# The borders between the passes of an FFT convolution: which PSUM slots and engines x's tiles use, and where they stand among the last transforms and modes

## Chip, cores and metric

One NeuronCore of a Trainium2 chip runs the kernel. The metric is device microseconds of one execution, the median over several runs. The kernel before takes 376.1 us (three runs: 375.57, 376.10 and 376.31).

## The reference, cut to what matters

x has shape (8, 5696, 128), h (5696, 128). The first half is a causal long convolution over the 5696 positions, by FFTs of length L = 2 * 5696; the second keeps 64 modes of the result's own FFT, mixes the 128 channels in each, transforms back, adds and passes a residual ReLU layer:

```python
Yf = np.fft.rfft(x, n=L, axis=1) * np.fft.rfft(h, n=L, axis=0)[None]
x = np.fft.irfft(Yf, n=L, axis=1)[:, :S, :]
X = np.fft.rfft(x, axis=1)[:, :64]                       # complex, 64 modes
Y = einsum('bmd,mde->bme', X, w_r + 1j * w_i)            # written in real parts
u = x + np.fft.irfft(Y, n=S, axis=1)
return u + np.maximum(u @ w_ch, 0.0)
```

## The kernel before

**The work.** The eight sequences are handled in four passes of two (`g_` from 0 to 3). The transform of length L is split into steps that are all matmuls. The *first transform* of a pass is 32 **tiles of x** (`a_tile`, line 466): tile j takes four channels, one matmul for each (128x180 out, constants F against x), into two neighbouring PSUM banks, a *slot* named by its lower bank (0, 2, 4 or 6). One eviction then copies the slot's 128x720 results to the SBUF tensor As, scaled by 1/64: on ScalarE (ACT; line 320 in the profile) or on VectorE (DVE; line 324). Tile 31 is evicted by both engines, half each.

Then the pass runs 23 **ticks** of four frequency columns (`ticks`; the last tick, 22, has two columns). A tick has the second transform (`second`, 128x128 matmuls ps<-As,M, which need all of As), the product with h's spectrum (`products`: mostly a copy Xs on ScalarE and a multiplication U on VectorE), and, two ticks later, the **third transform** (`third`, line 643): for each of the two sequences b two matmuls (ps<-U,Wc) into one bank and a copy Zs or Zt on ScalarE (line 318), then a DMA to the HBM scratch zscr on SP's queue. Its banks rotate through 4, 5 and 6 (`ZBANK`, with a counter `ring2["z"]` that runs on through the whole kernel). Three ticks later the **modes** (`modes_of`, line 660) accumulate small matmuls (ps<-G,Zs) into bank 7 (`MB`). After the last modes two ScalarE copies XT (lines 739 to 742) drain bank 7.

**The border** (lines 722 to 754). The tiles of the next pass can start when the second transform of the last tick is through. At the end of a pass transforms 21 and 22 (NT - 2 and NT - 1) and modes 20, 21 and 22 are still to be done. Before, PE's order is: transform 21 (both sequences), tiles 0 and 1 (slots 0 and 2), transform 22, tile 2 (slot 0), modes 20, tile 3 (slot 4), modes 21, tile 4 (slot 2), modes 22, XT, then tiles 5 to 31 in slots 0, 4, 6, 2 in turn. x itself is already in SBUF: it is loaded by DMA on POOL's queue during the ticks (`x_load`, to Xt) and rearranged by VectorE (`x_place`, line 371, Xin<-Xt), the last of eight in tick 22.

**Which engine evicts a tile** is chosen by `share` (line 435), a running balance of costs (670 ns for ScalarE, 815 for VectorE), with hand-set amounts added at the border. With V for VectorE and A for ScalarE it gives, for tiles 0 to 30, the same string at each border:

```
before  VAVVAVAVAVAVAVAAVAVAVAVAAVAVAVA
```

**What orders the work.** Every engine runs its instructions in the order in which the code records them. A `Recorder` derives the waits: a matmul into a bank waits for the eviction of what was in it, an eviction for the last matmul of its slot. After odd tiles from 5 on, one piece of the weights w_r, w_i is copied in HBM (wscr<-in_moe_w_r, 14 in a border) by a DMA on POOL's queue that waits for that tile's eviction; in the last border also loads W of those weights. Behind tile 31 PE runs nine matmuls on constants (`idle`), into slot 2.

Of the kernel before, what the change touches and what calls it, by code (L numbers as in the profile page):

```python
# [4 lines left out]
P = 128  # L5
# [118 lines left out]
def bass_long_conv_fft__then__afno_spectral_mix_kernel(nc, x, h, moe_w_r, moe_w_i, moe_w_ch, out):  # L124
# [10 lines left out]
    NT = (NK + KT - 1) // KT  # L135
# [156 lines left out]
    def ap(t, row, p0, n, off, dims):  # L292
        return bass.AP(t, p0 * row + off, [[row, n]] + [list(d) for d in dims])
# [5 lines left out]
    def pv(bank, off, dims, p0=0, n=P):  # L299
        return bass.AP(ps, p0 * 4096 + bank * 512 + off, [[4096, n]] + [list(d) for d in dims])  # L300
# [5 lines left out]
    def bank(i):  # L306
        return ("bank", i)
# [3 lines left out]
    def evac(dst, src, reads, writes, scale=None, eng=None, after=()):  # L311
        e = eng
        if e is None:
            turn[0] ^= 1
            e = "scalar" if turn[0] else "vector"
        if e == "scalar":
            if scale is None:
                R.add(e, lambda h_: h_.copy(dst, src), reads, writes, after=after)  # L318
            else:
                R.add(e, lambda h_: h_.activation(dst, src, COPY, scale=scale), reads, writes, after=after)  # L320
        elif scale is None:
            R.add(e, lambda h_: h_.tensor_copy(dst, src), reads, writes, after=after)  # L322
        else:
            R.add(e, lambda h_: h_.tensor_scalar_mul(dst, src, scale), reads, writes, after=after)  # L324

    def dma(eng, dst, src, ring, reads=(), writes=(), after=()):
        R.add(eng, lambda h_: h_.dma_start(dst, src), reads, writes, ring=ring, after=after)  # L327

    def mm(o, l, r, st, sp, reads, writes):
        R.add("tensor", lambda h_: h_.matmul(o, l, r, start=st, stop=sp), reads, writes)  # L330
# [3 lines left out]
    def once(key, toks):  # L334
        if key in first:
            return []
        first[key] = 1
        return list(toks)

    ring2 = {}  # L340

    def turns(name, items):
        i = ring2.get(name, 0)
        ring2[name] = i + 1
        return items[i % len(items)]
# [29 lines left out]
    def w_pieces():  # L375
        out_ = []
        for ri, w in ((0, moe_w_r), (1, moe_w_i)):
            for m0 in range(0, M, MWP):
                out_.append((bass.AP(wd, (ri * M + m0) * D, [[2 * M * D, P], [D, MWP], [1, D]]),
                             bass.AP(w.tensor, w.offset + m0 * D * D, [[D, P], [D * D, MWP], [1, D]]),  # L380
                             "w", ("wd", ri, m0)))
        return out_

    MWP = 4
    wp = w_pieces()
# [34 lines left out]
    ZBANK = [4, 5, 6]  # L420
# [4 lines left out]
    def idle(n, b0, w=512):  # L425
        for i in range(n):
            mm(pv(b0 + i % 2, 0, [[1, w]]), f1_sb[:, 0:P], ap(f1_sb, 2 * NK, 0, P, 0, [[0, w // P], [1, P]]),
               True, True, [("f1",)], [bank(b0 + i % 2)])
# [3 lines left out]
    load = {"scalar": 0.0, "vector": 0.0}  # L432
    COST = {720: (670, 815), 1024: (910, 1130), 256: (280, 330)}

    def share(n):
        a, v = load["scalar"] + COST[n][0], load["vector"] + COST[n][1]
        e = "scalar" if a <= v else "vector"
        load[e] = min(a, v)
        return e
# [26 lines left out]
    def a_tile(j, slots, eng=None):  # L466
        t = turns("s", slots) if len(slots) > 1 else slots[0]
        for i in range(4):
            d = 4 * j + i
            mm(pv(t + i // 2, (i % 2) * 2 * NK, [[1, 2 * NK]]),  # L470
               ap(x_sb, XW, 0, P, d // XD * XQ + d % XD, [[XE, 2 * J]]), f1_sb[:, :], True, True,
               XIN + XZ + [("f1",), ("xc", d // XD)], [bank(t + i // 2)])
        if eng == "both":
            for i, e in enumerate(("vector", "scalar")):
                evac(bass.AP(a_sb, 4 * j + 2 * i, [[AW, P], [D, 2 * NK], [1, 2]]), pv(t + i, 0, [[1, 2 * NK], [2 * NK, 2]]),
                     [bank(t + i)], [("as", j + i)], 1.0 / 64, eng=e, after=once(("hp", j), HP))
            return
        evac(bass.AP(a_sb, 4 * j, [[AW, P], [D, 2 * NK], [2, 2], [1, 2]]),
             pv(t, 0, [[1, 2 * NK], [512, 2], [2 * NK, 2]]),
             [bank(t), bank(t + 1)], [("as", j)], 1.0 / 64, eng=eng, after=once(("hp", j), HP))  # L480
# [24 lines left out]
    def load_g(i):  # L505
        s0, s1 = i * GP, min(i * GP + GP, NS)
        dma("sync", g_sb[:, s0 * P:s1 * P], bass.AP(c_g, s0 * P, [[GW, P], [1, (s1 - s0) * P]]), "c", (),
            [("g", i)], after=[("ag", k) for k in range(s0, s1)])
# [50 lines left out]
    V, A = "vector", "scalar"  # L559
# [77 lines left out]
    def zroom(g_, s_):  # L637
        return s_ % NZS[g_]
# [1 line left out]
    def xtok(n):  # L640
        return [("xt", n, p_) for p_ in range(2)]

    def third(g_, s_):
        if 0 <= s_ < NT:
            n = len(ticks[s_])
            i, zi = s_ % NU, zroom(g_, s_)
            zb = [turns("z", ZBANK) for b in range(2)]
            for b in range(2):
                for r in range(2):
                    mm(pv(zb[b], 0, [[1, n * D]]), (W1, W2)[r], u_s[i][:, r * 1024 + b * 512:r * 1024 + b * 512 + n * D],  # L650
                       r == 0, r == 1, [("u", i), ("wc",)] + ([("u0", i)] if s_ == 0 and b else []), [bank(zb[b])])
                evac(bass.AP(z_s[zi], b * D, [[1024, P], [2 * D, n], [1, D]]),
                     pv(zb[b], 0, [[D, n], [1, D]]), [bank(zb[b])], [("zs", zi, b)], eng="scalar",
                     after=once(("zx", zi, b), Z_OLD) if zi >= NZ else ())
            zo = (g_ * NK + KT * s_) * P * 256
            dma("sync", bass.AP(zs, zo, [[256, P], [P * 256, n], [1, 256]]),
                bass.AP(z_s[zi], 0, [[1024, P], [256, n], [1, 256]]), "z",
                [("zs", zi, 0), ("zs", zi, 1)], [("zd", g_, s_)])
# [48 lines left out]
    for j in range(32):  # L707
        a_tile(j, [turns("s", SLOTS)], "both" if j == 31 else share(720))
        if j >= 10 and j % 5 == 0:
            c_ = NE + (j - 10) // 5  # L710
            filter_couple(c_, turns("s", SLOTS), share(1024 if c_ + 1 < NH else 256))
    idle(8, turns("s", SLOTS), P)
    for g_ in range(NP):
        for t in range(NT + LM if g_ + 1 == NP else NT):
            if g_ == 0 and t % 2 == 0 and t // 2 < NG:
                load_g(t // 2)
            tick(g_, t)
            assert g_ + 1 < NP or not wp
            if g_ == NP - 1 and t in early:
                pace[:] = [("u", min(t, NT - 1) % NU)] if t else []  # L720
                early[t]()
        if g_ + 1 < NP:
            load.update(scalar=600.0, vector=0.0)
            third(g_, NT - 2)
            a_tile(0, [0], share(720))
            a_tile(1, [2], share(720))
            third(g_, NT - 1)
            load["scalar"] += 560.0
            a_tile(2, [0], share(720))
            modes_of(g_, NT - 3)  # L730
            a_tile(3, [4], share(720))
            modes_of(g_, NT - 2)
            a_tile(4, [2], share(720))
            modes_of(g_, NT - 1)
            load["scalar"] += 700.0
        if g_ + 1 == NP:
            reflect("vector", ib_sb, P, 2, ("ib",), M_ALL[0:6])
            reflect("vector", s4_sb[0], P, 0, ("s4", 0), M_ALL[2:8])
        evac(bass.AP(xt, 6 * g_ + 2, [[B * XTW, P], [3 * B, M], [2, 2], [1, 2]]), pv(MB, 0, [[1, M], [M, 2], [P, 2]]),
             [bank(MB)], [("xt", g_)], 1.0 / 64, eng="scalar", after=[("ag", k) for k in range(NS + 2 * XN, NK)])  # L740
        evac(bass.AP(xt, 6 * g_, [[B * XTW, P], [3 * B, M], [1, 2]]), pv(MB, M, [[1, M], [P, 2]]),
             [bank(MB)], [("xtn", g_)], -1.0 / 64, eng="vector" if g_ + 1 == NP else "scalar", after=[("ag", k) for k in range(NS + 2 * XN, NK)])
        if g_ + 1 < NP:
            for j in range(5, 32):
                a_tile(j, [(0, 4, 6, 2)[(j - 5) % 4]], "both" if j == 31 else share(720))
                if j == 31:
                    idle(9, 2, P)
                if wp and j % 2 == 1:
                    dst, src_, ring, tok = wp.pop(0)
                    dma("gpsimd", dst, src_, ring, (), [tok], after=[("as", j)])  # L750
                if g_ + 2 == NP:
                    for i in w_at.get(j, ()):
                        load_w(i)
# [192 lines left out]
```

## Time and profile before

| | us |
|---|---|
| median of three runs | 376.1 |
| the profiled execution | 375.71 |
| its span, first to last instruction | 373.9 |
| ticks of pass 1 (102.55 to 141.80) | 39.25 |
| border 1 (87.40 to 102.55) | 15.15 |
| border 2 (141.80 to 156.80) | 15.00 |
| border 3 (196.10 to 211.06) | 14.96 |
| last pass, drain and mixing (211.06 to 258.30) | 47.24 |
| output stage (258.30 to 373.90) | 115.60 |

All times in the profile are from the span's start, in one execution; the mean TensorE clock granted in it is 0.997. In the views a line has the start or the busy time, then engine, line of the code, operation and out<-in by the program's names. Because helpers record the instructions, line 330 is every matmul, 318, 320, 322 and 324 are evictions. A figure in brackets at a line's end is how long the engine stood idle before it, and who ended the idling. A merged line (x4) runs from the first one's start to the last one's end, and neighbours may overlap.

### The profile page before, as it was taken

What the parts mean: (1) busy time and instruction counts of PE and PEld (TensorE: products, weight loads), DVE (VectorE), ACT (ScalarE), POOL (GpSimd) and SP (SyncE); (2) the same over time, 40 slices, a digit from 0 to 9 for tenths busy, and PEclk for the clock granted to TensorE, in tenths of its full rate; (3) what the DMA queues carried; (4) which work ended last, traced back from release to release, by engine and by line L of the source; (5) the groups of instructions that cost most, each with busy time, mean ns of one, the idle gap of its engine ahead of it and who ended that gap; (6) DMA issues with size and microseconds to landing.
All of it is one profiled execution on the core that took longest, in us unless ns stands there. A gap on an engine that the chain in (4) does not pass through costs nothing.

```text
span 373.9 us, 12185 instructions
## 1 busy us (share of the span) xinstructions
PE 354.0 (95%) x5222; PEld 267.5 (72%) x5222; DVE 300.7 (80%) x333; ACT 312.2 (83%) x492; POOL 97.0 (26%) x140
## 2 busy tenths in 40 slices
PE   7989989999999999899999899999999999999993
PEld 3666866666856667766668666668898988898872
DVE  7686988998989998889998888782357776787784
ACT  8775989998989998999998899995466777777783
POOL 8765013220932312823204303318000000000000
PEclk9999999999999999999999999999999999999998
DMA  8998569998999996999996989999999999999768
GB/s 140 274 217 222 125 160 247 275 260 236 128 136 238 240 266 160 141 162 222 253 275 119 309 300 285 359 298 349 415 393 397 405 412 404 412 406 367 299 261 310
DMA packets 84130, 101.71 MB, mean 272 GB/s; under 512 B 22079, under 2 KB 68927, under 8 KB 81107
## 3 DMA queue, kind: packets, MB, share of 16 engines
q1 hardware_dynamic: 59643, 67.73, 52.9%
q0 software_dynamic: 24432, 33.20, 43.2%
q8 instruction: 41, 0.67, 0.7%
q14 instruction: 14, 0.11, 0.1%
HBM read 68.38 MB, written 51.12 MB: 320 GB/s over the span
## 4 chain that ended last, share of the span: by engine, by line
PE 79%; ACT 11%; DVE 4%; DMA 3%; issue 1%; DVEq 0%; POOL 0%; POOLq 0%
PE ps L330 78%; ACT As L320 7%; DMA Hin<-in_h_dram 3%; DVE As L324 1%; ACT R L880 1%; DVE U L623 1%; ACT UT L318 1%; ACT Hp L445 1%; DVE Ah L324 0%; DVE UT L322 0%; ACT Ah L320 0%; ACT XT L320 0%; DVE O L881 0%; ACT Hs L318 0%; DVE Os L881 0%
## 5 line engine op out<-in xcount | busy, mean ns | idle before, releaser
L330 PE MATMUL ps<-U,Wc 128*128 128x512 f16 (+1 forms) x368 | 94.6, 376 | 0.0
L631 DVE TENSOR_TENSOR U<-Xs,Hs 128x2048 f16<-128x2048 f16 (+1 forms) x68 | 80.5, 1188 | 11.1 <-ACT Xs L318 9.0
L318 ACT CAST Xs<-ps 128x1024 f16<-128x1024 f32 (+1 forms) x72 | 69.5, 971 | 6.9 <-PE ps L330 4.7
L881 DVE TENSOR_TENSOR O<-ps,R 128x512 f32<-128x512 f32 x81 | 52.5, 685 | 19.7 <-ACT R L880 11.2
L318 ACT CAST Zs<-ps 128x512 f16<-128x512 f32 (+1 forms) x120 | 63.0, 605 | 0.0
L880 ACT ACTIVATE R<-ps 128x512 f32<-128x512 f32 x96 | 50.9, 572 | 14.3 <-PE ps L330 13.9
L324 DVE TENSOR_SCALAR As<-ps 128x720 f16<-128x720 f32 (+1 forms) x65 | 53.9, 880 | 7.1 <-PE ps L330 6.1
L320 ACT ACTIVATE As<-ps 128x720 f16<-128x720 f32 (+1 forms) x67 | 47.4, 764 | 8.5 <-PE ps L330 7.8
L330 PE MATMUL ps<-F,Xin 128*128 128x180 f16 x512 | 51.9, 247 | 1.9 <-DVE As L324 0.8
L330 PE MATMUL ps<-As,M 64*128 64x128 f16 x1440 | 48.7, 217 | 4.8 <-DVE U L623 3.5
L330 PE MATMUL ps<-WI,UT 128*128 128x256 f16 x360 | 51.8, 278 | 0.5 <-DVE O L881 0.4
L330 PEld LDWEIGHTS ps<-F,Xin 128*128 128x128 f16 x512 | 43.2, 142 | 9.8 <-DVE As L324 4.5
L330 PEld LDWEIGHTS ps<-U,Wc 128*128 128x128 f16 x368 | 28.2, 97 | 29.1 <-ACT Zs L318 6.2
L330 PEld LDWEIGHTS ps<-As,M 64*128 64x128 f16 x1440 | 40.3, 94 | 10.6 <-DVE U L623 4.1
L631 DVE TENSOR_TENSOR U<-ps,Hs 128x2048 f16<-128x2048 f32 x20 | 45.7, 2283 | 0.0
L327 POOL DMA_DIRECT2D Xt<-in_x_dram x48 | 24.8, 520 | 75.5 <-PE ps L330 74.9
L318 ACT CAST UT<-ps 128x712 f16<-128x712 f32 x40 | 30.0, 752 | 16.7 <-PE ps L330 15.9
L330 PEld LDWEIGHTS ps<-WI,UT 128*128 128x128 f16 x360 | 39.3, 152 | 4.2 <-issue 1.9
L330 PE MATMUL ps<-IBs,C 128*128 128x356 f16 x128 | 39.2, 314 | 0.8
L330 PEld LDWEIGHTS ps<-G,Zs 128*128 128x128 f16 x468 | 25.7, 96 | 12.0
L318 ACT CAST Zt<-ps 128x512 f16<-128x512 f32 (+1 forms) x64 | 33.8, 604 | 0.3 <-DMA zscr<-Zt 0.2
L322 DVE CAST UT<-ps 128x712 f16<-128x712 f32 x24 | 21.4, 891 | 9.5 <-PE ps L330 9.5
(90 smaller groups left out, 505.8 us busy)
## 6 DMA issues: line engine op xcount, KB each, us to landing
out_dram<-O SPq DMA_DIRECT2D x39, 512.0 KB, 7.5
zscr<-Zs SPq DMA_DIRECT2D x57, 256.0 KB, 6.3
zscr<-Zt SPq DMA_DIRECT2D x31, 256.0 KB, 8.1
Xt<-in_x_dram POOLq DMA_DIRECT2D x24, 320.0 KB, 6.8
W<-wscr POOLq DMA_DIRECT2D x8, 512.0 KB, 8.7
ZT0a<-zscr SPq DMA_DIRECT2D x3, 1024.0 KB, 9.4
Xr<-in_x_dram POOLq DMA_DIRECT2D x8, 320.0 KB, 16.5
M<-cM POOLq DMA_DIRECT2D x3, 720.0 KB, 13.1
```

The costliest lines, as they stand in the source:

```text
L318: R.add(e, lambda h_: h_.copy(dst, src), reads, writes, after=after)
L320: R.add(e, lambda h_: h_.activation(dst, src, COPY, scale=scale), reads, writes, after=after)
L322: R.add(e, lambda h_: h_.tensor_copy(dst, src), reads, writes, after=after)
L324: R.add(e, lambda h_: h_.tensor_scalar_mul(dst, src, scale), reads, writes, after=after)
L327: R.add(eng, lambda h_: h_.dma_start(dst, src), reads, writes, ring=ring, after=after)
L330: R.add("tensor", lambda h_: h_.matmul(o, l, r, start=st, stop=sp), reads, writes)
L445: R.add("scalar", lambda e, dst=dst, src=src: e.copy(dst, src), HT, [("hp", c_)])
L623: R.add("vector", lambda e, b=b, s_=s_: e.tensor_tensor(bass.AP(u_s[i], b * 512, [[2048, P], [1024, 2], [1, n * D]]), s_, hv, MULT), [tok, ...
L631: R.add("vector", lambda e: e.tensor_tensor(uv, src, hv, MULT), bk + [("h", t, 0), ("h", t, 1, 0), ("h", t, 1, J)], [("u", i)])
L880: R.add("scalar", lambda e: e.activation(rv, src_r, RELU), bk, [("r", i % NR)], after=once(("r", i % NR), G_ALL + XTT + [("y", q) for q in ...
L881: R.add("vector", lambda e: e.tensor_tensor(ov, src_u, rv, ADD), bk + [("r", i % NR)], [key + (h_,)], after=once(key, old))
```

## The change

- `third` takes the sequences that it is to do (`bs`). At a border transform 21's first sequence is issued alone, then tile 0, then the second sequence, whose call issues the DMA.
- The tiles have fixed slots: 2, 0, 2, 4 for tiles 0 to 3, then 0, 2, 4, 6 in turn.
- They have fixed engines, 16 of the 31 whole tiles on ScalarE as before:

```
after   VVAVVAAVAVAVAVAAVAVAVAAVAVAVAVA
```

- Tile 4 moves behind modes 22: PE's order is transform 21 first half, tile 0, second half, tile 1, transform 22, tile 2, modes 20, tile 3, modes 21, modes 22, XT, tiles 4 to 31.
- The transforms' bank counter is set to 2 at the start of each pass, so that every border has transform 21 in banks 6 and 4, and transform 22 in 5 and 6.
- The nine constant matmuls behind tile 31 go into slot 0.

```diff
-    def third(g_, s_):
+    def third(g_, s_, bs=(0, 1)):
...
-            zb = [turns("z", ZBANK) for b in range(2)]
-            for b in range(2):
+            zb = {b: turns("z", ZBANK) for b in bs}
+            for b in bs:
...
+            if 1 not in bs:
+                return
...
+    BSLOT = [2, 0, 2, 4] + [0, 2, 4, 6] * 7
+    BENG = "VVAVVAAVAVAVAVAAVAVAVAAVAVAVAVA"
+
+    def border_tile(j):
+        a_tile(j, [BSLOT[j]], "both" if j == 31 else {"V": "vector", "A": "scalar"}[BENG[j]])
+
     for g_ in range(NP):
+        ring2["z"] = 2
...
         if g_ + 1 < NP:
-            load.update(scalar=600.0, vector=0.0)
-            third(g_, NT - 2)
-            a_tile(0, [0], share(720))
-            a_tile(1, [2], share(720))
+            third(g_, NT - 2, (0,))
+            border_tile(0)
+            third(g_, NT - 2, (1,))
+            border_tile(1)
             third(g_, NT - 1)
-            load["scalar"] += 560.0
-            a_tile(2, [0], share(720))
+            border_tile(2)
             modes_of(g_, NT - 3)
-            a_tile(3, [4], share(720))
+            border_tile(3)
             modes_of(g_, NT - 2)
-            a_tile(4, [2], share(720))
             modes_of(g_, NT - 1)
-            load["scalar"] += 700.0
...
-            for j in range(5, 32):
-                a_tile(j, [(0, 4, 6, 2)[(j - 5) % 4]], "both" if j == 31 else share(720))
+            for j in range(4, 32):
+                border_tile(j)
                 if j == 31:
-                    idle(9, 2, P)
-                if wp and j % 2 == 1:
+                    idle(9, 0, P)
+                if wp and j > 4 and j % 2 == 1:
```

## The prediction, made before the changed kernel ran

> **What bounds the kernel now.** I read the page first (busy shares and the chain that ended last), then the chain piece by piece around one border, then the timelines of ScalarE (ACT), VectorE (DVE) and TensorE (PE) there. "Border" is the stretch between two of the four passes. Tick 21 and tick 22 are a pass's last two (the code's NT - 2 and NT - 1).
>
> The page, its line of busy times and the shares of the chain by engine:
>
> ```profile
> span 373.9 us, 12185 instructions
> ...
> PE 354.0 (95%) x5222; PEld 267.5 (72%) x5222; DVE 300.7 (80%) x333; ACT 312.2 (83%) x492; POOL 97.0 (26%) x140
> ...
> PE 79%; ACT 11%; DVE 4%; DMA 3%; issue 1%; DVEq 0%; POOL 0%; POOLq 0%
> ```
>
> PE carries 79% of the chain, and the change removes no matmul from it, so it can only win where the chain leaves PE. The chain in order of time (start, length, what) says where:
>
> ```profile
> 87.86 0.92 DVE As L324
> ...
> 88.83 1.95 PE ps L330 x28
> ...
> 90.80 0.78 ACT As L320
> 91.58 0.45 ACT XT L320 x2
> ...
> 92.48 0.92 DVE As L324
> ...
> 93.45 1.66 PE ps L330 x16
> ...
> 95.13 7.41 ACT As L320 x11
> ...
> 104.53 37.69 PE ps L330 x580
> ...
> 142.24 0.92 DVE As L324
> ...
> 143.21 1.82 PE ps L330 x28
> ...
> 149.39 7.41 ACT As L320 x11
> ...
> 196.50 0.92 DVE As L324
> ...
> 203.65 7.40 ACT As L320 x11
> ```
>
> Each border runs over evictions: VectorE's tile 0, back to PE, ScalarE's tile 4 and XT, VectorE's tile 7, then eleven ScalarE copies in a row. After that PE runs 37.69 us without leaving the chain. The first border's copies end at 95.13 + 7.41 = 102.54. From tile 0's copy to that end it is 14.68 us (102.54 - 87.86); in the second (156.80 - 142.24) and the third (211.05 - 196.50) 14.56 and 14.55.
>
> The stretch of the first border by engine, then ScalarE and VectorE at its opening:
>
> ```profile
> 87.40:102.55 15.15, 14.28 (x162) 12.22 (x160) 13.27 (x17) 13.64 (x23) 9.14 (x13) 1.00 1.07 159
> ```
> ```profile
> 85.75 0.62 ACT L318 CAST Xs<-ps 128x512 f16<-128x512 f32 x1
> 86.23 2.10 ACT L318 CAST Zs<-ps 128x512 f16<-128x512 f32 x4
> 88.17 0.83 ACT L320 ACTIVATE As<-ps 128x720 f16<-128x720 f32 x1
> 88.84 0.70 ACT L318 CAST Zs<-ps 128x256 f16<-128x256 f32 x2
> 90.80 0.78 ACT L320 ACTIVATE As<-ps 128x720 f16<-128x720 f32 x1 [1.25 <-PE ps L330]
> 91.46 0.55 ACT L320 ACTIVATE XT<-ps 128x256 f16<-128x256 f32 x2
> ```
> ```profile
> 86.15 0.68 DVE L371 COPY Xin<-Xt 89x2048 f16<-89x2048 f16 x1
> 86.75 0.68 DVE L631 TENSOR_TENSOR U<-Xs,Hs 128x1024 f16<-128x1024 f16 x1
> 87.86 0.91 DVE L324 TENSOR_SCALAR As<-ps 128x720 f16<-128x720 f32 x1 [0.43 <-PE ps L330]
> 89.39 1.72 DVE L324 TENSOR_SCALAR As<-ps 128x720 f16<-128x720 f32 x2 [0.62 <-PE ps L330]
> ```
>
> In 15.15 us ScalarE works 13.64 and VectorE 13.27, at clock 1.00: the two evicting engines are the limit, and they lose 1.5 and 1.9 us. The losses are at the opening: ScalarE idles 1.25 us before tile 4, VectorE 0.43 and 0.62 before tiles 0 and 2, all waiting for PE. What the change can win is this idle time.
>
> **The change part by part.** Unit costs first, PE's, then the copies':
>
> ```profile
> 86.39 1.13 PE L330 MATMUL ps<-U,Wc 128*128 128x512 f16 x4
> 87.35 0.78 PE L330 MATMUL ps<-F,Xin 128*128 128x180 f16 x8
> ...
> 88.83 0.53 PE L330 MATMUL ps<-F,Xin 128*128 128x180 f16 x4 [0.26 <-DVE As L324]
> ...
> 90.28 0.47 PE L330 MATMUL ps<-F,Xin 128*128 128x180 f16 x4
> 90.60 0.33 PE L330 MATMUL ps<-G,Zs 128*128 128x4 f16 x4
> 90.76 1.09 PE L330 MATMUL ps<-F,Xin 128*128 128x180 f16 x10
> ```
> ```profile
> L320 ACT ACTIVATE As<-ps x17: 531/775/831, 88.2 to 102.0; 128x720 f16<-128x720 f32 x16, 128x360 f16<-128x360 f32 x1
> L324 DVE TENSOR_SCALAR As<-ps x16: 539/898/908, 87.9 to 101.9; 128x720 f16<-128x720 f32 x15, 128x360 f16<-128x360 f32 x1
> ```
> ```profile
> 91.89 10.65 ACT L320 ACTIVATE As<-ps 128x720 f16<-128x720 f32 x15
> ```
> ```profile
> 92.48 9.93 DVE L324 TENSOR_SCALAR As<-ps 128x720 f16<-128x720 f32 x12 [0.30 <-PE ps L330]
> ```
>
> A tile's four matmuls take 0.47 us to the end of the last, 0.53 after a wait, and hold PE for 0.31 (eight in 0.78 are 0.08 apart). A transform half is two matmuls of 0.38, 0.22 apart: 0.60, PE held 0.43. Four matmuls of the modes hold it 0.16 (90.60 to 90.76). PE goes on 0.06 after an eviction's end (87.86 + 0.91, then 88.83). A copy takes ScalarE 0.78, and the next starts 0.69 later (eleven copies in 7.41, the last, a half tile, 0.53: ten starts in 6.88). VectorE: 0.90, next after 0.82 (two in 1.72).
>
> Nothing is added or removed: the same 32 tiles, the same 16 to ScalarE and 15 to VectorE with tile 31 halved, the same 14 weight copies on POOL's queue, the same order on SP's. Instructions move on PE, ScalarE and VectorE alone. Now the first border with the new order, on before's clock:
>
> 1. Transform 21's first half starts on PE at 86.39, as now; PE is free at 86.82. Tile 0 goes to banks 2 and 3, free since ScalarE's copy ended at 86.37. It needs the last placement of x (86.15 + 0.68 = 86.83): so 86.89, done 87.42. VectorE ends its product at 87.43 and copies tile 0 at **87.44, against 87.86**.
> 2. The price: the half behind it starts at 87.25 instead of 86.92 (the four end at 86.39 + 1.13), so its copy starts at 87.87 instead of 87.67 (the last of the four in 2.10 us, 0.48 apart). Behind it on ScalarE stand only transform 22's copies, which gain from the next step.
> 3. Tile 1 (banks 0 and 1, long free) goes to VectorE instead of ScalarE: done 88.15, copied 88.26 to 89.16. ScalarE, without its 0.83 us copy between, does transform 22's copies from 88.40 to 89.09, against 88.84 to 89.54.
> 4. Tile 2 waits for tile 0's banks (88.34): done 88.92, on ScalarE at 88.94. That is work in the hole of 1.25 us.
> 5. Modes of tick 20 (eight matmuls, 0.33), tile 3 (banks 4 and 5, whose transform copies ended at 88.51 and 88.84), modes of 21 and 22 behind it, twelve matmuls in 0.5. Tile 3 is done at 89.55, on VectorE at 89.57 after 0.5 idle: the one hole that stays. The modes end at 90.05, so XT runs 90.07 to 90.63, **against 91.46 to 92.01**. Here the move of tile 4 behind the modes pays: ScalarE waits 0.4 for them instead of 1.25 for tile 4, and tile 7, which needs XT's bank, is freed 1.4 earlier.
> 6. Tile 4 done 90.35, VectorE at 90.39. Tile 5 done 90.66, ScalarE at 90.68. Tile 6 waits for tile 3's banks (90.47), ScalarE at **91.35, against 91.89**. Tile 7 done 91.36, VectorE at **91.38, against 92.48**.
>
> From here the work left is that of before: tile 6 is the third full tile of ScalarE in both orders, tile 7 the fifth of VectorE in both. Before, ScalarE took 10.65 - 0.53 = 10.12 us for the fourteen starts behind tile 6, 0.72 each. The first four came 0.81 apart (91.89 to 95.13), since their tiles stood on PE behind VectorE's late ones (the chain goes 92.48 VectorE, PE, 95.13 ScalarE); then 0.69. With VectorE 1.10 ahead that delay has no cause left, so I take 0.69 throughout: 91.35 + 14 x 0.69 + 0.53 = **101.54, against 102.54**. VectorE keeps its 9.93 us for tiles 7 to 31: 91.38 + 9.93 = 101.31, no longer later than ScalarE.
>
> **Sum.** First border 1.00 us. The other two are 0.12 and 0.13 shorter already: the piece of PE from tile 2 to tile 4 takes 1.82 us there instead of 1.95, because tile 3 doesn't wait for a bank of the transforms, whose rotation differs by pass. The change starts that rotation at the same place in every pass, so all three come out alike: 1.00 + 0.88 + 0.87 = 2.75 us. Behind a border nothing waits for the clock: the pass is PE's, and what POOL issues hangs on tiles and ticks, so it moves along. The profiled execution took 375.71 us (span 373.9, 1.8 outside it): 373.0. It lies 0.39 under the median of 376.1 of three runs; the median less 2.75 is **373.3 us**.
>
> Bounds: below, ScalarE keeps 0.72 after tile 6 and only its 0.54 there stays: 0.54 + 0.42 + 0.41 = 1.4 us, 374.7. Above, VectorE's 1.10 is all that it can give: 1.10 + 0.98 + 0.97 = 3.05, 373.05. I stay by 0.69 because ten starts in a row measured it in all three borders.
>
> [...]
>
> **The rivals.**
> [...]
> - *Half the gain.* ScalarE stays coupled to PE at 0.72, 374.7 as bounded above. For it: slots are still reused every four tiles, and a pair of ScalarE tiles in a row (5 and 6, 14 and 15, 21 and 22) holds PE up. Against it: after 95.13 the same coupling gave 0.69. Chance 15%.
> - *The gain is given back in the pass*, by a wait that the profile hides behind the border: about 376.1. Against it: the chain runs 37.69 us on PE in each pass. Chance 6%.
> - *Slower: x arrives late.* Tile 0 now stands on PE ahead of half a transform and waits for the last placement of x, for which x's last load must have landed. Loads and placements of the second pass's end:
>
> ```profile
> L371 DVE COPY Xin<-Xt x4: 679/682/683, 131.8 to 140.5; 89x2048 f16<-89x2048 f16 x4
> L327 POOL DMA_DIRECT2D Xt<-in_x_dram x3: 510/517/527, 129.6 to 132.9; - x3
> ...
> DMA to landing us min/median/max: 5.4/6.9/7.1
> ```
>
>   The last is issued at 132.9, lands by 140.0 and is placed at 140.5, 0.5 us of cover. If the weight copies of a shorter border ran further into the pass and pushed that landing back, every us beyond 0.5 would cost a us in each of three passes. From 1.7 us on (1.2 beyond, 3.6 in all, less 2.75) the kernel is slower by over 0.2%; at 2 us it takes 376.1 - 2.75 + 4.5 = 377.9. Against it: the weight copies hang on the same tiles as the end of the border, so they end as far into the pass as now. Chance 8%.
>
> **How the numbers follow.** Forecast 68%, with gains of 2.3 to 3.1 us (373.0 to 373.8, and 0.4 either way for the scatter of medians, whose three runs span 375.57 to 376.31). Rivals 3, 15, 6 and 8%. The range reaches from 372.4 to the half-gain case with its scatter, 375.0; that holds 83%. Faster by over 0.2% (0.75 us, about what a measurement of this kernel can tell from no change): 68 + 15 = 83%. Within 0.2%: 3 + 6 = 9%. Slower: 8%.
>
> **What would show it.** In the profile after: VectorE's first border copy at once behind its last product; no wait of ScalarE over 0.6 us before tile 5; XT 1.4 us earlier against tile 0's old start; the fourteen starts behind tile 6 in 9.5 to 9.8 us; three borders of equal length, each 15.15 us from transform 21's first matmul to the last copy's end (now 102.54 - 86.39 = 16.15 in the first). [...]

## The result, and the profile after

The changed kernel takes 373.39 us (median of six runs, 373.02 to 374.75) against 376.21 us before (six runs, 375.57 to 376.72): ratio 0.9923, 95% interval 0.9904 to 0.9943. Measured again later beside other runs of before it was 374.31 against 376.06, ratio 0.9953, interval 0.9935 to 0.9972. So it is faster by 0.5 to 0.8%, and the forecast of 373.3 us is 0.1 off the first median and 1.0 off the second. What the profile shows of the gain is 2.35 us (a ratio of 0.9937, which lies in both intervals).

The profiled execution took 373.66 us. Its page, the lines that were shown of before:

```profile
span 371.9 us, 12188 instructions
...
PE 353.4 (95%) x5222; PEld 268.0 (72%) x5222; DVE 300.6 (81%) x333; ACT 312.5 (84%) x492; POOL 97.2 (26%) x140
...
PE 79%; ACT 13%; DMA 3%; DVE 2%; issue 1%; DVEq 0%; POOL 0%; POOLq 0%
```

The engines do the same work in a shorter span. On the chain ScalarE has risen and VectorE fallen. The chain in order of time shows how:

```profile
49.44 40.78 PE ps L330 x624
...
90.24 10.86 ACT As L320 x16
...
101.15 0.67 PE ps L330 x16
101.82 1.23 DVE U L623
...
103.09 36.83 PE ps L330 x574
...
143.76 10.88 ACT As L320 x16
...
197.29 10.86 ACT As L320 x16
```

Before, a border went from VectorE to PE, ScalarE, XT, PE, VectorE and PE before ScalarE's last eleven copies. Now PE runs through, from the pass right into the border, until tile 5 is in its slot (XT is drained just before); then ScalarE copies its last sixteen pieces without a break (15 starts in 10.86 - 0.53 = 10.33 us, 0.69 each).

The border's opening on ScalarE and on VectorE:

```profile
85.20 0.62 ACT L318 CAST Xs<-ps 128x512 f16<-128x512 f32 x1
85.67 2.90 ACT L318 CAST Zs<-ps 128x512 f16<-128x512 f32 x6
88.50 0.78 ACT L320 ACTIVATE As<-ps 128x720 f16<-128x720 f32 x1
89.62 0.56 ACT L320 ACTIVATE XT<-ps 128x256 f16<-128x256 f32 x2 [0.35 <-PE ps L330]
```
```profile
85.60 0.68 DVE L371 COPY Xin<-Xt 89x2048 f16<-89x2048 f16 x1
86.20 0.68 DVE L631 TENSOR_TENSOR U<-Xs,Hs 128x1024 f16<-128x1024 f16 x1
86.97 1.72 DVE L324 TENSOR_SCALAR As<-ps 128x720 f16<-128x720 f32 x2
89.13 2.75 DVE L324 TENSOR_SCALAR As<-ps 128x720 f16<-128x720 f32 x3 [0.44 <-PE ps L330]
```

ScalarE's wait of 1.25 us has become one of 0.35, and VectorE's 0.43 and 0.62 have become 0.44 once. Tile 0's copy starts 0.09 us behind VectorE's last product (86.88), tile 2 is copied by ScalarE where it had idled.

To compare kernels I measure a border from the start of x's last placement (the Xin<-Xt line) to the first second-transform matmul behind it (ps<-As,M, where the chain names PE again). The first border here is 101.15 - 85.60 = 15.55 us; before it was 102.59 - 86.15 = 16.44. All three: 16.44, 16.30, 16.30 before and **15.55, 15.58, 15.56** after. That is 0.89 + 0.72 + 0.74 = 2.35 us. The two passes between the borders take 37.95 us each in both profiles. The span fell by only 2.0 us, because this execution was 0.55 us earlier at the first border and 0.84 us longer behind the last one (163.67 against 162.83 us); the last section shows how far that stretch scatters.

### The profile page after: what moved, and what is told of

It is laid out like the page before. It is cut to its first block, busy times and chain, and to the rows that moved or that the text cites. A ratio compares the mean times of both kernels' runs of the same rounds, so it can differ in the third digit from the quotient of the medians.

```text
span 371.9 us, 12188 instructions
## 1 busy us (share of the span) xinstructions
PE 353.4 (95%) x5222; PEld 268.0 (72%) x5222; DVE 300.6 (81%) x333; ACT 312.5 (84%) x492; POOL 97.2 (26%) x140
## 4 chain that ended last, share of the span: by engine, by line
PE 79%; ACT 13%; DMA 3%; DVE 2%; issue 1%; DVEq 0%; POOL 0%; POOLq 0%
PE ps L330 79%; ACT As L320 9%; DMA Hin<-in_h_dram 3%; DVE U L623 1%; ACT R L886 1%; ACT UT L318 1%; ACT Hp L445 1%; DVE Ah L324 0%; DVE UT L322 0%; ACT Ah L320 0%; ACT Hs L318 0%; DVE O L887 0%; DVEq L105 0%; POOL Hin L327 0%; ACT C L320 0%
## 5 line engine op out<-in xcount | busy, mean ns | idle before, releaser
L320 ACT ACTIVATE As<-ps 128x720 f16<-128x720 f32 (+1 forms) x67 | 46.3, 763 | 4.3 <-PE ps L330 4.0
```

## The experiments

The theory: up to XT a border is PE's sequence, behind XT it is ScalarE's remaining copies at 0.69 us as long as VectorE is ahead; order and engine string each bring a part. The rivals are that the string alone, the order alone, the moved modes or the slots make the gain. The changed kernel's borders repeat to 0.03 us, while its two medians are 0.9 us apart (373.39 and 374.31; before has 376.06 to 376.37), so the borders are the finer measure. Each ratio in the table is to runs of before that were taken beside that kernel.

| kernel | borders, us | median, us | ratio to before, 95% interval |
|---|---|---|---|
| before | 16.44, 16.30, 16.30 | 376.07 | |
| changed | 15.55, 15.58, 15.56 | 373.39 | 0.9923 (0.9904 to 0.9943) |
| changed, again | 15.57, 15.58, 15.55 | 374.31 | 0.9953 (0.9935 to 0.9972) |
| new order, old string | 15.82, 15.83, 15.82 | 374.53 | 0.9977 (0.9950 to 1.0004) |
| old order, new string | 16.04, 16.03, 16.02 | 375.23 | 0.9973 (0.9958 to 0.9988) |
| transform 21 unsplit | 15.91, 15.91, 15.91 | 374.88 | 0.9961 (0.9946 to 0.9976) |
| tile 4 between modes 21 and 22 | 15.69, 15.70, 15.70 | 373.87 | 0.9937 (0.9915 to 0.9959) |
| rotation not reset | 15.64, 15.56, 15.55 | 373.84, one run | |
| old slots | 15.52, 15.49, 15.51 | 374.17, one run | |
| old slots, again | 15.51, 15.50, 15.49 | 373.95 | 0.9941 (0.9929 to 0.9953) |
| one tile from ScalarE to VectorE | 16.35, 16.34, 16.36 | 376.73 | 1.0015 (0.9998 to 1.0032) |
| tile 3 ahead of modes 20 | 15.54, 15.57, 15.55 | 374.11 | 0.9941 (0.9923 to 0.9959) |
| old slots, another string | 15.46, 15.44, 15.45 | 373.44 | 0.9926 (0.9913 to 0.9938) |

**The new order with the old engines.**

```diff
-    BENG = "VVAVVAAVAVAVAVAAVAVAVAAVAVAVAVA"
+    BENG = "VAVVAVAVAVAVAVAAVAVAVAVAAVAVAVA"
```

> The changed kernel with the engine string of before (VAVVAVAV...); order, slots and bank rotation as changed. Border length is taken from the start of x's last placement (VectorE, Xin<-Xt) to the first second-transform matmul behind the border (ps<-As): before 16.44, 16.30, 16.30 us; changed 15.55, 15.58, 15.56. Theory (PE's sequence up to XT and then ScalarE's remaining tiles set the end; order and engines both count): tile 1 stands on ScalarE in front of transform 22's copies and delays tile 2 and tile 3's bank; the step-by-step walk of the prediction, repeated with this string, ends 0.39 us later: 15.95 per border, 1.2 us over the changed kernel, 374.6. Rival 'engines': the string alone makes the gain, so it is gone here: 16.3 per border, about 376. Rival 'order': the placement alone makes it: 15.56, 373.4.

Measured: 15.82 per border, 0.13 under the theory's 15.95 and far from both rivals. (The time alone can't tell it from before: its interval reaches 1.0004.) ScalarE, then VectorE, at the opening of its first border:

```profile
88.14 0.78 ACT L320 ACTIVATE As<-ps 128x720 f16<-128x720 f32 x1
88.80 0.66 ACT L318 CAST Zs<-ps 128x256 f16<-128x256 f32 x2
90.13 0.56 ACT L320 ACTIVATE XT<-ps 128x256 f16<-128x256 f32 x2 [0.67 <-PE ps L330]
```
```profile
87.23 0.91 DVE L324 TENSOR_SCALAR As<-ps 128x720 f16<-128x720 f32 x1
88.75 1.80 DVE L324 TENSOR_SCALAR As<-ps 128x720 f16<-128x720 f32 x2 [0.62 <-PE ps L330]
90.75 3.35 DVE L324 TENSOR_SCALAR As<-ps 128x720 f16<-128x720 f32 x4 [0.20 <-PE ps L330]
```

Tile 1 stands before transform 22's copies on ScalarE again, and VectorE's 0.62 is back. ScalarE's third tile starts almost as early as in the changed kernel (5.37 us after the placement's start, there 5.32), but VectorE's fifth 0.35 later (5.72, 5.37). From ScalarE's third tile to its end, here and then in the changed kernel:

```profile
91.23 10.40 ACT L320 ACTIVATE As<-ps 128x720 f16<-128x720 f32 x15
```
```profile
90.92 10.18 ACT L320 ACTIVATE As<-ps 128x720 f16<-128x720 f32 x15
```

Less the last half tile's 0.53 these are 9.87 us for fourteen starts, and 9.65 in the changed kernel. Before had 10.12, with the engine string of this run. VectorE's fifth copy starts 0.6 us behind ScalarE's third before, 0.35 here and 0.05 in the changed kernel, and the first four of ScalarE's fourteen starts take 3.24, 3.00 and 2.80 us; the other ten take 6.85 to 6.88 in all three. That is the coupling that the prediction claimed for before: how late VectorE's tiles are sets ScalarE's pace, over four copies.

**The new engines with the old order.** The kernel before, with each `share(720)` of a border replaced by the new string's engine:

```diff
-            a_tile(0, [0], share(720))
-            a_tile(1, [2], share(720))
+            a_tile(0, [0], eng_of(0))
+            a_tile(1, [2], eng_of(1))
...
```

> The kernel before with the new engine string alone; order, slots and rotation as before. Theory: the same walk gives 0.44 us less than before in the first border and 0.31 in the other two, 16.0 each: 1.05 us faster than before, 375.1. Rival 'engines': 15.56 per border, 373.4. Rival 'order': 16.44, 16.30, 16.30, 376.2.

Measured: 16.04, 16.03, 16.02, as the theory had it; both rivals are out. VectorE and ScalarE at the opening:

```profile
86.13 0.68 DVE L371 COPY Xin<-Xt 89x2048 f16<-89x2048 f16 x1
86.73 0.68 DVE L631 TENSOR_TENSOR U<-Xs,Hs 128x1024 f16<-128x1024 f16 x1
87.85 1.72 DVE L324 TENSOR_SCALAR As<-ps 128x720 f16<-128x720 f32 x2 [0.43 <-PE ps L330]
```
```profile
89.38 0.77 ACT L320 ACTIVATE As<-ps 128x720 f16<-128x720 f32 x1 [0.35 <-PE ps L330]
90.82 0.57 ACT L320 ACTIVATE XT<-ps 128x256 f16<-128x256 f32 x2 [0.67 <-PE ps L330]
```

The 0.43 before tile 0 stays, which only the order removes. The string alone is worth 0.40, 0.27 and 0.28 us in the three borders, the order with slots and rotation alone 0.62, 0.47 and 0.48. Together they would be 1.02, 0.74 and 0.76; the changed kernel has 0.89, 0.72 and 0.74. They add up but for 0.13 us in the first border and 0.02 in the others.

**Transform 21 in one piece.**

```diff
-            third(g_, NT - 2, (0,))
+            third(g_, NT - 2)
             border_tile(0)
-            third(g_, NT - 2, (1,))
             border_tile(1)
```

> The changed kernel with transform 21 in one piece and tile 0 behind it. Theory: tile 0 comes 0.43 us later to VectorE, whose copies of tiles 0 and 1 free the banks of tiles 2 and 4; the walk ends 0.47 us later: 16.03 per border, 1.4 us over the changed kernel, 374.8. Rival: the split is paid back by the later second half (0.2 us later on ScalarE) and is worth nothing: 15.56, 373.4.

Measured: 15.91 in each border, 0.35 lost instead of 0.47. VectorE in the first border:

```profile
86.55 0.69 DVE L371 COPY Xin<-Xt 89x2048 f16<-89x2048 f16 x1
87.15 0.68 DVE L631 TENSOR_TENSOR U<-Xs,Hs 128x1024 f16<-128x1024 f16 x1
88.27 1.72 DVE L324 TENSOR_SCALAR As<-ps 128x720 f16<-128x720 f32 x2 [0.43 <-PE ps L330]
```

The split is worth 0.35 us a border, over a third of the gain. Tile 0 is copied 1.72 us after the placement's start here, 1.37 in the changed kernel and 1.29 in the prediction: the 0.08 by which the forecast was too early is most of what the expectation overrated.

**Tile 4 back between the modes.**

```diff
             modes_of(g_, NT - 2)
+            border_tile(4)
             modes_of(g_, NT - 1)
...
-            for j in range(4, 32):
+            for j in range(5, 32):
```

> The changed kernel with tile 4 back between modes 21 and modes 22. Theory: XT comes later by the 0.31 us that the tile holds PE, ScalarE's tiles behind it by half of that; the walk ends 0.14 us later: 15.70 per border, 0.4 us over the changed kernel, 373.8. Rival 'modes': the move of tile 4 is what makes the gain (XT was 1.3 us earlier after the change): XT back at 5.2 us after the placement's start, 16.2 per border, 375.4 or more.

Measured: 15.70, to the hundredth. So the move of tile 4 behind the modes is the smallest of the three parts (the split, the string, this move), 0.14 us a border. XT does come 0.32 later (4.34 us after the placement's start, against 4.02), but ScalarE then finds its next tile ready, and its third tile starts only 0.11 later.

**Rotation and slots.** First the reset is left out, then the slots are those of before; each ran once.

```diff
-        ring2["z"] = 2
```

> The changed kernel without the reset of the transforms' bank counter. Theory: only the first border is touched (there transform 21 then stands in banks 4 and 5, and tile 3 waits for transform 22's later copy): 0.12 us longer, 15.67, the other two 15.56; the time is that of the changed kernel within 0.2. Rival: the rotation makes no difference in any border.

```diff
-    BSLOT = [2, 0, 2, 4] + [0, 2, 4, 6] * 7
+    BSLOT = [0, 2, 0, 4, 2] + ([0, 4, 6, 2] * 7)[:27]
...
-                    idle(9, 0, P)
+                    idle(9, 2, P)
```

> The changed kernel with the slots of before (0, 2, 0, 4, 2, then 0, 4, 6, 2 in turn; constants into slot 2). Theory: tile 0 waits for the placement and not for its banks, and every slot is reused at the same distance, so nothing changes: 15.56 per border within 0.05. Rival 'slots': the fixed slots carry part of the gain: 15.8 or more.

Measured: without the reset 15.64, 15.56, 15.55, so it saves 0.09 us, once. With the old slots 15.52, 15.49, 15.51: the new slots gain nothing and cost 0.05. The reason shows in the old slots' first border, VectorE and then tile 0 on PE (weight loads, matmuls), beside tile 0 in the changed kernel:

```profile
86.42 0.68 DVE L371 COPY Xin<-Xt 89x2048 f16<-89x2048 f16 x1
```
```profile
87.16 0.35 PEld L330 LDWEIGHTS ps<-F,Xin 128*128 128x128 f16 x4 [0.40 <-DVE Xin L371]
87.16 0.53 PE L330 MATMUL ps<-F,Xin 128*128 128x180 f16 x4
```
```profile
86.40 0.35 PEld L330 LDWEIGHTS ps<-F,Xin 128*128 128x128 f16 x4 [0.47 <-ACT Zs L318]
86.43 0.50 PE L330 MATMUL ps<-F,Xin 128*128 128x180 f16 x4
```

In slot 0 tile 0 waits for the placement alone and starts 0.06 us after its end (87.10). In slot 2 its first matmul waits for VectorE and for ScalarE's copy out of that slot, and its weights are loaded 0.12 after the placement's end (86.28), its matmul starts at 86.43, 0.15 after. ScalarE's copy had ended at 85.82. The last section shows what stands between.

**One tile from ScalarE to VectorE.** Tile 28, late in the border:

```diff
-    BENG = "VVAVVAAVAVAVAVAAVAVAVAAVAVAVAVA"
+    BENG = "VVAVVAAVAVAVAVAAVAVAVAAVAVAVVVA"
```

> The changed kernel with tile 28 on VectorE instead of ScalarE, 15 to 16. Theory (both evicting engines are full from XT to the end, VectorE 0.1 us behind ScalarE): VectorE ends one copy, 0.75 to 0.82 us, later: 16.3 per border, 2.2 us over the changed kernel, 375.6. Rival (ScalarE's pace alone sets the end, VectorE has room): ScalarE ends one copy earlier, 14.9 per border, 371.4. Rival (PE sets the pace by its waits): no difference.

Measured: 16.35 per border, 0.78 more, the whole gain gone (ratio 1.0015). VectorE and ScalarE at the first border's end:

```profile
97.97 4.63 DVE L324 TENSOR_SCALAR As<-ps 128x720 f16<-128x720 f32 x6 [0.16 <-PE ps L330]
```
```profile
96.58 3.52 ACT L320 ACTIVATE As<-ps 128x720 f16<-128x720 f32 x5
100.72 1.15 ACT L320 ACTIVATE As<-ps 128x720 f16<-128x720 f32 x2 [0.62 <-PE ps L330]
```

VectorE ends at 102.60 and ScalarE, with a tile less, at 101.87. "ScalarE alone sets the end" and "PE sets the pace" both fall: the two engines are full together (in the changed kernel they end at 100.99 and 101.10), and a single tile too many on VectorE costs as much as a border gained. A tile too many on ScalarE was not tried.

**Tile 3 ahead of modes 20.**

```diff
             border_tile(2)
-            modes_of(g_, NT - 3)
             border_tile(3)
+            modes_of(g_, NT - 3)
             modes_of(g_, NT - 2)
```

> The changed kernel with tile 3 ahead of modes 20 instead of behind them. Theory: VectorE's wait before tile 3 (0.44 us) shrinks by up to 0.3 and comes back before tile 4; XT stays where it is, and with it ScalarE and the end: 15.56 per border, 373.4 within 0.2. Rival: VectorE's hole is what is left to win: 15.35 per border, 372.8.

Measured: 15.54, 15.57, 15.55. VectorE:

```profile
87.24 2.75 DVE L324 TENSOR_SCALAR As<-ps 128x720 f16<-128x720 f32 x3
90.21 1.84 DVE L324 TENSOR_SCALAR As<-ps 128x720 f16<-128x720 f32 x2 [0.22 <-PE ps L330]
```

All but 0.1 us of the hole before tile 3 is gone, and 0.22 of it is back before tile 4; XT stays at 4.02 us. VectorE's hole is not what is left to win.

**The changed kernel again, the old slots timed, and another string.** In the third, tile 2 too goes to VectorE:

```diff
-    BENG = "VVAVVAAVAVAVAVAAVAVAVAAVAVAVAVA"
+    BENG = "VVVAVAVAAVAVAVAAVAVAVAVAAVAVAVA"
```

> The changed kernel again, with more runs. Theory (the whole gain is made at the three borders: 0.89 + 0.72 + 0.74 = 2.35 us by the first profile): ratio .9937 to before, 2.35 us, and in the profile three borders of 15.56 us and two passes of 37.95. Rival (something behind the borders gains too, since the median fell by 2.82): ratio .9925 or less again.

> The changed kernel with the slots of before, timed. In its one look the borders were 15.52, 15.49 and 15.51 us, 0.05 shorter, because tile 0's first matmul waited for VectorE alone and started 0.06 us behind the placement instead of 0.15. Theory: 15.51 again, 0.15 us in all, which the time can't show: ratio to before within 0.001 of the changed kernel's. Rival: the slots do matter elsewhere: over 0.5 us apart.

> The changed kernel with the slots of before and another string, VVVAVAVAAVAVAVAAVAVAVAVAAVAVAVA, the best that the step-by-step walk found for this order (tile 2 on VectorE too, so that ScalarE is through earlier). Theory: 0.05 from the wait of tile 0 and 0.07 from the string: 15.44 per border, 0.36 us under the changed kernel in all. Rival (nothing is left, since PE up to XT and ScalarE behind it are both without holes): 15.51 as with the slots alone, or longer.

Measured: the changed kernel's borders and passes repeat within 0.03 us; the interval of its ratio, 0.9935 to 0.9972, holds the theory's 0.9937, at its edge, and not the rival's 0.9925. With the old slots 15.50, as in their first run. With the other string too 15.45, as the walk had it: 0.34 us under the changed kernel by the borders. Its time, 373.44, is the lowest of these three, and its interval overlaps with the old slots' and the changed kernel's. So a version that is better in the trace exists, by 0.1% of the time, which these runs can't resolve.

## Why the prediction was right

**The bound.** Right: what could be won was the evicting engines' idle time at the opening. ScalarE's waits on PE there fell from 1.25 to 0.35 us and VectorE's from 1.05 to 0.44, and the passes kept 37.95 us. The view of the first border before also has PE busy for 14.28 of its 15.15 us, more than either evicting engine, which the prediction passed over; that PE's work is not the limit was shown by one tile from ScalarE to VectorE, which leaves that work as it is and lengthens the border by 0.78.

**The steps, from the placement's start** (86.15 before, 85.60 after). The forecast's times are in brackets. Tile 0's copy starts at 1.37 (1.29), tile 2's at 2.90 (2.79), tile 3's at 3.53 (3.42), XT at 4.02 (3.92), tile 5's at 4.64 (4.53), tile 6's on ScalarE at 5.32 (5.20), tile 7's on VectorE at 5.37 (5.23). Every step is 0.08 to 0.14 us later than it was put. **The step that missed is the first one**, "so 86.89, done 87.42": tile 0 started 0.15 us after the placement, not 0.06, because in its new slot it waits for two engines, one of them long done. The old slots, with one wait, bring 0.06 back at every step from tile 0 to tile 7. The other 0.03 to 0.08 come in behind tile 0, half of it by tile 2; no run separates them.

**The price of the split.** Right: transform 21's second half is later (it starts 0.93 us behind the first half's start, against 0.52 in the kernel before) and nothing came of it; unsplit, the border is 0.35 longer.

**The pace of 0.69.** Right, and the term on which most hung: 9.65 us for the fourteen starts behind tile 6 (forecast 9.66; 10.12 before). That VectorE's lead is what frees it was shown by the old string under the new order, where the same string as before's took 9.87 with VectorE 0.25 less behind. One copy lasts 0.78 us, and the next starts before it ends: behind XT there are 15 starts in 10.33 us.

**Three alike.** Right: 15.55, 15.58, 15.56; without the reset the first is 0.09 longer. From transform 21's first matmul to the last copy's end the first border takes 15.26 us (101.10 - 85.84), where the forecast had 15.15.

**The sum.** By the borders 0.89 + 0.72 + 0.74 = 2.35 us against 1.00 + 0.88 + 0.87 = 2.75. The forecast's first 1.00 was 0.54 from tile 6's earlier start on ScalarE and 0.46 from the pace behind it; measured it was 0.42 and 0.47. So what is missing, 0.11 to 0.16 us a border, lies before tile 6, and 0.03 to 0.08 of it goes with the new slots. Taken out of the changed kernel one at a time, the split, the string and the move of tile 4 cost 0.35, 0.26 and 0.14 us a border and the new slots give back 0.05: 0.70 in all, of 0.72 and 0.74 in the later borders. The medians' difference was 2.82 us in the first measurement, which fits 2.75 better than the trace does, and 1.75 in the second, which fits it worse; both are scatter about 2.35. The forecast's median came out to 0.1 us partly by luck.

**The rivals.** *Half the gain* fell with the pace. Of the chances, the 3% was for ScalarE's copies following each other more slowly even with VectorE ahead; no run shows that, and in the changed kernel they came 0.69 apart (14 starts in 9.65 us). *Given back in the pass* fell with 37.95 us in both kernels. *x arrives late* did not happen: no placement waited in the changed kernel, whose group of all 24 shows an idle time of 0.0:

```profile
L371 DVE COPY Xin<-Xt 89x2048 f16<-89x2048 f16 x24 | 16.4, 682 | 0.0
```

How much later x would have to land was not tried.

## What to carry to other kernels

Where two engines evict and both are nearly full, look for their idle time in the few us where the previous stage's last work is still in the queues, and interleave there: a tile between the halves of a transform, and on the engine whose queue is empty, was worth more (0.35 and 0.26 us a border here) than the position of the modes (0.14). Walk such a stretch instruction by instruction with durations and start-to-start distances from the trace; here that gave every step to 0.14 us. Keep the number of engines that a first instruction waits for in view: moving tile 0 to another slot added a second wait and cost 0.05 us a border. Compare variants by the length of the stretch in the trace, which repeats to 0.03 us here, when the whole time's median differs by 0.9 between two measurements of one kernel.

## What the runs showed of the hardware

**A matmul with two waits started later.** Tile 0's first matmul started 0.15 us after the later of its two releasers, against 0.06 with that one wait alone. In the changed kernel PE's queue (PEldq) has a semaphore instruction of its own between the transform's half and tile 0's weights:

```profile
L115 PEldq EVENT_SEMAPHORE  x1: 51/51/51, 86.3 to 86.3; - x1
```

It waits for VectorE: it starts at 86.32, 0.04 us after the placement's end, and takes 0.05; the weights, whose load carries the other wait, follow 0.03 behind it, and the matmul 0.03 behind their start. With the old slots there is no such instruction in front of tile 0: the load itself carries the one wait, and starts 0.05 after the placement's end. The profile names ScalarE's following copy as the releaser, but that copy ended at 86.31, before the semaphore instruction did. The delay is the same in all three borders of every profile: with tile 0 between the halves its first matmul starts 0.83 us after the placement's start in slot 2 (seven profiles), and 0.74 in slot 0 (three).

**Where a part of the whole time's scatter comes from.** The changed kernel's two profiles differ by 2.0 us in the span (371.9 and 373.9), 1.1 of it before the first border and 0.9 behind the last. In the list of waits, PE's waits on "issue" (for nothing that the profile shows; total us, times, longest us), of before, of the changed kernel and of the changed kernel again:

```profile
PE ps L330 <- issue: 0.7, 1, 0.7
```
```profile
PE ps L330 <- issue: 1.1, 2, 0.7
```
```profile
PE ps L330 <- issue: 2.3, 3, 1.2
```

One such wait, of 0.4 to 1.3 us, stands near 29 us in all thirteen profiles; before has no other. A second one stands at 327 to 330 us, in the output stage, in four of them: 0.68 us in the changed kernel, 1.23 in the changed kernel again. These four have the longest stretches behind the last border, 163.67 to 164.56 us; the other nine have 162.28 to 163.60 (before 162.83). So such a wait is a part of the scatter and not all of it, and what makes PE wait was not found out.
